# Plain block of an FNet/MLP kernel: first real round on the bare layer norm, scale and shift of the modulation at its eviction

## Chip, core and metric

One core of one Trainium2 chip runs the whole program. The metric is device time in microseconds (us). The kernel before took 1977.84 us, the median of three runs (1975.1 to 1978.34). TensorE is PE, VectorE DVE, ScalarE ACT, GpSimd POOL; SP is the queue that issues most loads.

## What is computed

x is 2048 tokens by 1024 channels; everything is float32 outside.

```python
mod = (_silu(c) @ w_mod).reshape(c.shape[0], 6, 1, -1)
sa, ca, ga, sb, cb, gb = (mod[:, 0], ..., mod[:, 5])
h = _layernorm(x, axis=-1) * (1 + ca) + sa
# _A_ref: a = h @ dft_hid_re.T, b = h @ dft_hid_im.T
#         y = dft_seq_re @ a - dft_seq_im @ b
x = x + ga * _A_ref(h, A_dft_seq_re, A_dft_seq_im, A_dft_hid_re, A_dft_hid_im)
h = _layernorm(x, axis=-1) * (1 + cb) + sb
x = x + gb * _B_ref(h, B_w1, B_b1, B_w2, B_b2)   # gelu MLP, 1024 -> 3584 -> 1024
```

The kernel takes the sequence transform first, so its first products are dft_seq_re times h and dft_seq_im times h.

## The kernel before

Each float32 operand of a product is split into two float16 parts, hi (a rounding, done by ACT) and lo (the rest, done by DVE), and every product is three float16 matmuls: hi by hi, hi by lo, lo by hi (`PASSES`). The stages are: modulation row and layer norm of x; the sequence transform for the first 512 output tokens as a plain block (L1133, `plain1`); the other three groups of 512 tokens by a Strassen-Winograd scheme with seven products (L1183, `winograd1`); the hidden transform (L1415); and the MLP (L1613, L1722).

The plain block is 16 steps. Steps n = 0 to 7 are the real matrix, 8 to 15 the imaginary one. A step uses row tiles k and k+8 of h (k = n % 8) and one coefficient tile, `cop(n)`, and makes 48 matmuls of 128x512: 8 channel groups d (one PSUM bank each), 2 row tiles s, 3 passes. After step 7 the eight banks are evicted by ACT into `uf` (L1112), after step 15 again. Later the kernel needs sums of h tiles for the Winograd scheme (`s_tasks`): four DVE operations (L668 to L671), then hi by ACT (L679) and lo by DVE (L682), stored to DRAM by POOL (L686) from a ring of two buffers, so that the hi of one pair waits for the store of the pair before it.

Before the plain block can begin, h is needed, and h needs sa and ca, that is 8 MB of w_mod. So the program starts with eight loads of 1 MB (L1448). Four of the eight contributions go through PE as float32 matmuls (L485, L507) and four through DVE (L491, L493, summed by L1489); matmuls without use keep PE busy between them (L501). `mod_rows` takes the maximum of the row (L528), makes a power-of-two scale from it and applies it with ca and sa to the first tile. All other tiles go through `x_tasks`: sums by ACT (L622) and squares by ACT (L626), a chain of small operations (L624 to L639), then x minus mean times ca (DVE, L654), times the inverse deviation plus sa (DVE, L655), hi (ACT, L656), lo (DVE, L657). Coefficient tiles are loaded at L713 and split at L702 (ACT) and L705 (DVE). The rows ga, sb, cb, gb are made later (`row_tasks`, L563, L565).

The order on each engine is fixed when the program is built: a planner with costs and due times (`push(stream, tag, tasks, due)`) picks the next task, and each engine then runs its queue in order, stopping wherever an operand isn't there.

## Time and profile before

| | us |
|---|---|
| median of three runs | 1977.84 |
| the profiled execution, its own time | 1974.14 |
| span in the profile | 1972.4 |
| first matmul of the plain block | 34.55 |
| first matmul of the Winograd stage | 208.99 |
| PE busy / DVE busy / ACT busy | 1955.6 / 1421.8 / 851.9 |

PE is the engine to follow: the time is the work of PE and the stretches in which it has none. A busy share of 99% hides two things. Before 34.55 PE is counted as busy with matmuls whose results are thrown away. And matmuls overlap, so that the duration of one (379 ns) is not what it costs; in an undisturbed stretch one starts every 0.216 us.

### The profile page before, as it was taken

What the parts mean: (1) busy time and instruction counts of PE and PEld (TensorE: products, weight loads), DVE (VectorE), ACT (ScalarE), POOL (GpSimd) and SP (SyncE); (2) the same over time, 40 slices, a digit from 0 to 9 for tenths busy, and PEclk for the clock granted to TensorE, in tenths of its full rate; (3) what the DMA queues carried; (4) which work ended last, traced back from release to release, by engine and by line L of the source; (5) the groups of instructions that cost most, each with busy time, mean ns of one, the idle gap of its engine ahead of it and who ended that gap; (6) DMA issues with size and microseconds to landing.
All of it is one profiled execution on the core that took longest, in us unless ns stands there. A gap on an engine that the chain in (4) does not pass through costs nothing.

```text
span 1972.4 us, 23659 instructions
## 1 busy us (share of the span) xinstructions
PE 1955.6 (99%) x9040; PEld 890.5 (45%) x9040; DVE 1421.8 (72%) x1800; ACT 851.9 (43%) x1091; POOL 195.9 (10%) x287
## 2 busy tenths in 40 slices
PE   8999999999999999999999999999999999999999
PEld 3444444444444444444444444444444444444443
DVE  5977888797984477776689998989873453553566
ACT  4743332344542255554576566556323412312311
POOL 0012212221210012211020000000000000000000
PEclk9999999999999999999999999999999999999999
DMA  9158587598788868878954454445476432432324
GB/s 385 63 166 268 184 313 279 211 334 316 252 288 330 304 230 264 279 237 305 353 166 150 187 192 167 151 142 183 175 219 192 125 102 72 133 102 65 113 75 86
DMA packets 139362, 402.41 MB, mean 204 GB/s; under 512 B 15536, under 2 KB 15536, under 8 KB 134640
## 3 DMA queue, kind: packets, MB, share of 16 engines
q1 hardware_dynamic: 111808, 307.30, 46.3%
q0 software_dynamic: 27440, 93.60, 13.3%
q8 instruction: 70, 1.15, 0.2%
q14 instruction: 44, 0.36, 0.1%
HBM read 262.95 MB, written 137.89 MB: 203 GB/s over the span
## 4 chain that ended last, share of the span: by engine, by line
PE 91%; DVE 4%; DMA 2%; ACT 1%; issue 1%; SPq 0%; POOL 0%; DVEq 0%; ACTq 0%; POOLq 0%
PE ps L1613 24%; PE ps L1183 22%; PE ps L1722 22%; PE ps L1415 15%; PE ps L1133 8%; DMA arena<-in_x_dram 1%; DVE arena L409 1%; DVE arena L1768 1%; PE ps L1317 1%; DVE arena L422 1%; ACT arena L397 1%; DMA arena<-in_w_dram 1%; DVE arena L1812 0%; DMA zc<-arena 0%; SPq L1448 0%
## 5 line engine op out<-in xcount | busy, mean ns | idle before, releaser
L1722 PE MATMUL ps<-arena 128*128 128x512 f16 x2352 | 511.3, 379 | 3.4 <-ACT arena L1758 1.4
L1613 PE MATMUL ps<-arena 128*128 128x512 f16 x2352 | 510.4, 379 | 0.0
L1183 PE MATMUL ps<-arena 128*128 128x512 f16 x2016 | 435.3, 379 | 0.0
L1722 PEld LDWEIGHTS <-arena 128*128 128x128 f16 x2352 | 229.9, 98 | 282.5 <-issue 4.8
L1613 PEld LDWEIGHTS <-arena 128*128 128x128 f16 x2352 | 230.2, 98 | 277.0 <-issue 0.3
L1768 DVE SCALAR_TENSOR_TENSOR arena<-ps,i4c,arena 128x1024 f32<-128x1024 f32 x179 | 229.4, 1281 | 145.1 <-PE ps L1722 142.2
L1183 PEld LDWEIGHTS <-arena 128*128 128x128 f16 x2016 | 197.3, 98 | 237.8
L1415 PE MATMUL ps<-arena 128*128 128x512 f16 x1344 | 292.2, 379 | 0.0
L397 ACT ACTIVATE arena<-arena,shc 128x512 f16<-128x512 f32 (+1 forms) x115 | 116.1, 1018 | 281.9 <-PE ps L1722 189.2
L1415 PEld LDWEIGHTS <-arena 128*128 128x128 f16 x1344 | 131.5, 98 | 155.9
L1133 PE MATMUL ps<-arena 128*128 128x512 f16 x768 | 170.1, 384 | 6.5 <-ACT arena L538 2.1
L422 DVE TENSOR_TENSOR arena<-arena 128x512 f32<-128x512 f32 (+1 forms) x228 | 171.0, 753 | 4.2
L702 ACT ACTIVATE arena<-arena 128x1024 f16<-128x1024 f32 x100 | 103.8, 1050 | 155.6 <-PE ps L1183 101.4
L409 DVE SCALAR_TENSOR_TENSOR arena<-arena,shc 128x512 f16<-128x512 f32 (+1 forms) x115 | 128.7, 1122 | 37.4 <-ACT arena L397 37.1
L705 DVE SCALAR_TENSOR_TENSOR arena<-arena 128x1024 f16<-128x1024 f32 x100 | 132.2, 1339 | 26.4 <-ACT arena L702 26.2
L1639 DVE TENSOR_TENSOR arena<-arena,ps 128x512 f32<-128x512 f32 x84 | 57.6, 685 | 109.8 <-PE ps L1613 107.1
L1632 ACT ACTIVATE arena<-arena,b1s,i1c 128x512 f32<-128x512 f32 x84 | 68.3, 813 | 137.6 <-DVE arena L1639 137.6
L1133 PEld LDWEIGHTS <-arena 128*128 128x128 f16 x768 | 75.6, 99 | 100.9 <-issue 6.4
L794 ACT ACTIVATE arena<-arena 128x1024 f16<-128x1024 f32 x56 | 57.4, 1047 | 51.2 <-DMA u<-arena 18.7
L797 DVE TENSOR_TENSOR arena<-arena 128x1024 f16<-128x1024 f32 x56 | 66.9, 1220 | 15.4 <-ACT arena L794 15.4
L397 ACT ACTIVATE arena<-arena,s1c 128x512 f16<-128x512 f32 (+1 forms) x70 | 60.7, 884 | 37.8 <-DVE arena L422 26.2
L409 DVE SCALAR_TENSOR_TENSOR arena<-arena,s1c 128x512 f16<-128x512 f32 (+1 forms) x70 | 66.4, 959 | 10.8 <-ACT arena L397 10.8
(169 smaller groups left out, 1400.2 us busy)
## 6 DMA issues: line engine op xcount, KB each, us to landing
w<-arena SPq DMA_DIRECT2D x64, 512.0 KB, 4.9
arena<-w SPq DMA_DIRECT2D x119, 256.0 KB, 2.7
u<-arena POOLq DMA_DIRECT2D x56, 512.0 KB, 5.4
arena<-u SPq DMA_DIRECT2D x112, 256.0 KB, 3.9
arena<-w SPq DMA_DIRECT2D x56, 512.0 KB, 3.5
arena<-s SPq DMA_DIRECT2D x48, 512.0 KB, 6.4
arena<-in_cre_dram SPq DMA_DIRECT2D x32, 512.0 KB, 7.5
...
```

What stands on the lines that cost most here:

```text
L397: act.activation(o[m][0], q(j), AF.Copy, **sc)
L409: dve.scalar_tensor_tensor(o[m][1], q(j), scale, o[m][0], op0=ALU.mult, op1=ALU.subtract)
L422: dve.tensor_tensor(q(d), q(a), q(b), op=op)
L702: h = Task("act", 1.15, lambda: act.activation(o[:, :, 0], s2, AF.Copy, scale=SC), list(deps) + free)
L705: dve.scalar_tensor_tensor(o[:, :, 1], s2, SC, o[:, :, 0], op0=ALU.mult, op1=ALU.subtract)
L1133: pe.matmul(bank_of(d_), hleft(d_, s, kp, a), cop(n)[:, s, b], start=(kp == 0 and s == 0 and a == 0 and b == 0), stop=(kp == 7 and s == 1 ...
L1183: pe.matmul(bank_of(st + ch), left, cop(n)[:, s, b], start=(start and kp == 0 and s == 0 and a == 0 and b == 0), stop=(kp == 3 and s == 1 ...
L1415: pe.matmul(bank_of(bk), up(N)[:, c_, a], dp(n)[:, c_, w], start=(start and ri == 0 and c_ == 0 and i == 0), stop=(ri == 1 and c_ == 3 and ...
L1613: pe.matmul(ps.rearrange("p (k t) -> p k t", k=4), w1c[:, m, s, a, d * P : (d + 1) * P], zc(m)[:, b, :, d, :], start=(start and d == 0 and ...
L1632: act.activation(dst, src, AF.Gelu_apprx_tanh, scale=inv, bias=b1s[:, 2 * p + j : 2 * p + j + 1])
L1722: pe.matmul(t[:, j], hidc[:, c_, m, a, k * P : (k + 1) * P], w2c[:, m, c_, w], start=(start and c_ == 0 and n == 0), stop=(c_ == 1 and n = ...
L1768: lambda: dve.scalar_tensor_tensor(dst, ps[b], inv, dst, op0=ALU.mult, op1=ALU.add), kp[b],
```

## The change

The first real round works on the bare layer norm, LN(x) times 1024, instead of on h. Since h = LN(x) (1+ca) + sa and the channels are the rows of the result, the product for one channel is (1+ca) times the product with LN(x), plus sa times the sum of the coefficients over the 2048 input positions. So the eviction of the real round scales each partition by a column of 1+ca (`cols`, `evict_plain`), and then DVE adds the coefficient sums times a column of sa (`shift_tasks`). The imaginary round and the Winograd stage still use h. In detail:

- Loads begin with x and coefficient tiles; the eight 1 MB loads of w_mod lie between them (`head`, `tail`), in four buffers.
- All eight contributions of w_mod are summed by DVE (`wm_tasks`); four float32 matmuls with ones, in bank 7, add over the partitions (`mod_sum`) during the real round. Bank 7 is therefore used for d = 7 only after that: the real round runs d = 0 to 6 for all eight steps (42 matmuls each), then d = 7 for all eight (6 each).
- `x_tasks` no longer waits for the row: it normalises x in one operation, on ACT for ten tiles (`ACT_N`), on DVE for six; hi and lo follow.
- New `h_tasks` makes h from LN(x) during the imaginary round: times ca, plus sa, hi, lo for all 16 tiles.
- Eight accumulating loads on POOL sum the coefficients (`csum_tasks`), and two float32 matmuls add over partitions in step 8.
- sa and ca go through DRAM to become columns (`rc_d`, `cols`): 2048 elements of 4 bytes.
- Due times of the later streams move; the loads of `row_tasks` get a stream of their own.

```diff
     def cop(n):
-        return at(O_OP + 4 * (n % 6), 2048, F16).rearrange(...)
+        o = O_OP + 4 * (n % 6 if n < 6 else (n - 8) % 6) if n not in (6, 7) else O_AUX + 12 + 4 * (n - 6)
+        return at(o, 2048, F16).rearrange(...)
...
+    def wm_tasks(k):
+        t = []
+        for h in (1, 0):
+            p = slice(h * D, h * D + D)
+            def f(p=p):
+                if k == 0:
+                    dve.tensor_scalar(rows[:, p], wm2(k)[:, p], scol[:, k : k + 1], None, op0=ALU.mult)
+                else:
+                    dve.scalar_tensor_tensor(
+                        rows[:, p], wm2(k)[:, p], scol[:, k : k + 1], rows[:, p], op0=ALU.mult, op1=ALU.add
+                    )
...
+    def mod_sum(h, n):
...
+        p = rows[:, h * D + 512 * n : h * D + 512 * n + 512]
+        pe.matmul(bank_of(7), ones[:, 0:P], p, start=True, stop=True)
+        t = [Task("act", 0.6, lambda: act.activation(p, bank_of(7), AF.Copy, bias=float(h)), ...)]
...
+    def mod_tasks():
+        t = chain(
+            ("dve", 2.3, lambda: dve.tensor_reduce(mx, rows, axis=AX.X, op=ALU.max, apply_absolute_value=True)),
...
+            ("dve", 0.75, lambda: dve.tensor_scalar(ca1s, rows[:, D : 2 * D], sh, 1.0 / SX, op0=ALU.mult, op1=ALU.mult)),
+            ("dve", 0.75, lambda: dve.tensor_scalar(sas, rows[:, 0:D], sh, None, op0=ALU.mult)),
...
+        a = Task("dma", 1.0, lambda: sp.dma_start(rc_d[:, :], scaled[0:1, :]), ["mod"], "rcs")
+        b = Task("dma", 1.0, lambda: sp.dma_start(cols, rc_d[0].rearrange("(r c p) -> p r c", r=2, p=P)), ["rcs"], "rcl")
...
+    def csum_tasks():
+        for k in range(8):
+            kw = {"accum_op": ALU.add} if k else {}
+            f = lambda k=k, kw=kw: gp.dma_start(csum, cre[0, :, k::8, :], **kw)
...
+    ACT_N = {(4, 0), (7, 1), (3, 1), (6, 1), (7, 0), (5, 1), (3, 0), (5, 0), (6, 0), (4, 1)}
...
+            u = chain(
+                by_act(x_, cl[:, 2, n : n + 1], r) if (k, n) in ACT_N
+                else ("dve", 0.8, lambda: dve.tensor_scalar(x_, x_, mean, r, op0=op, op1=ALU.mult)),
+                ("act", 1.15, lambda: act.activation(hv[:, :, 0], x2, AF.Copy)),
+                ("dve", 1.23, lambda: dve.tensor_tensor(hv[:, :, 1], x2, hv[:, :, 0], op=ALU.subtract)),
+            )
...
+    def h_tasks(k):
-                ("dve", 1.3, lambda x_=x_, mean=mean, op=op: dve.scalar_tensor_tensor(x_, x_, mean, ca1s, op0=op, op1=ALU.mult)),
-                ("dve", 1.3, lambda x_=x_, n=n: dve.scalar_tensor_tensor(x_, x_, r[:, n : n + 1], sas, op0=ALU.mult, op1=ALU.add)),
+                ("dve", 1.23, lambda x_=x_: dve.tensor_tensor(x_, x_, ca1s, op=ALU.mult)),
+                else ("dve", 1.23, lambda x_=x_: dve.tensor_tensor(x_, x_, sas, op=ALU.add)),
...
-    T0 = 42.0
+    T0 = 11.0
...
-        sc = (1.0 - 2.0 * ri) * 2.0**-16
+        sc = -(2.0**-16) if ri else cols[:, 1, d : d + 1]
...
+    def shift_tasks():
+        t = [Task("act", 0.6, lambda: act.activation(rsum, bank_of(7), AF.Copy), ["rs"], "rsum")]
+        for d in range(ND):
+            f = lambda o=o, s=s: dve.scalar_tensor_tensor(o, rsum, s, o, op0=ALU.mult, op1=ALU.add)
...
-                push("u", "u", u_tasks(tb, 0, [[("ev", tb, 1)], [("ev", tb, 6)]]), clk["pe"] + 25.0)
+                push("u", "u", u_tasks(tb, 0, [[("ev", tb, 1)], [("ev", tb, 6)]]), clk["pe"] + -15)
...
+    head = "x0 x8 c0 x1 x9 c1 x2 x10 c2 w0 w1".split()
+    tail = "x3 x11 c3 w2 w3 x4 x12 c4 w4 w5 x5 x13 c5 w6 w7 x6 x14 c6 x7 x15 c7".split()
+    idle_pe(24)
...
-        push("s", "s", s_tasks(k), t_op(8) + 8.0 * k)
+        push("hm", "hm", ab[0], t_op(8 + k) - 25)
+        push("h", "h", ab[1], t_op(8 + k) - 20)
+        push("s", "s", s_tasks(k), T1 - 70 + 7 * k)
...
-    ... row_tasks(...), t_op(16) + 20.0 + 30.0 * n)
+    ... row_tasks(...), t_op(16) + 60.0 + 30 * n)
-        push("row", "row", d_tasks(n), t_op(16 + 28) + 24.0 * n)
+        push("row", "row", d_tasks(n), t_op(16 + 28) + 40 + 22 * n)
```

How the queues change is shown at three places. The line numbers are those of the kernel that a row belongs to. In the changed kernel L496 and L498 are the w_mod products, L652 the layer norm statistics of the first two tiles, L635 the normalisation on DVE and L627 on ACT, L636 hi and L637 lo of LN(x), L667 sums and L671 squares, L744 and L747 hi and lo of the coefficients, L692 and L694 times ca and plus sa, L695 and L696 hi and lo of h, L710 to L713 the four operations of `s_tasks` and L724 its lo, L839 a later split (`u_tasks`).

DVE, from the start of the program, before:

```order
L491 TENSOR_SCALAR arena_65<-arena_65,scol_186 128x2048
L493 SCALAR_TENSOR_TENSOR arena_65<-arena_65,scol_186 128x2048 x2
L493 SCALAR_TENSOR_TENSOR arena_65<-arena_65,scol_186 128x1024 x2
L613 BN_STATS xst_7_190<-arena_65 128x6 x2
L615 BN_AGGR xmv_9_192<-xst_7_190 128x2
```

DVE now, from the normalisation of tile 8 (the fourth operand that PE waits for) on:

```order
L635 TENSOR_SCALAR arena_65<-arena_65,xmv_9_193,xcl_10_194 128x1024
L669 TENSOR_SCALAR xcl_12_196<-xmv_11_195 128x2
L496 TENSOR_SCALAR arena_65<-arena_65,scol_186 128x1024
L637 TENSOR_TENSOR arena_65<-arena_65 128x2x512
L747 SCALAR_TENSOR_TENSOR arena_65<-arena_65 128x2x512
L673 TENSOR_SCALAR xcl_12_196<-xmv_11_195 128x2
L496 TENSOR_SCALAR arena_65<-arena_65,scol_186 128x1024
L617 RECIPROCAL xcl_12_196<-xcl_12_196 128x2
```

The statistics have moved ahead of the w_mod products, and those now stand between the operations of the tiles: the lo of tile 8 (the first L637 here) stands behind the first half product of w_mod.

ACT, in the stretch in which row tiles 5, 13, 6 and 14 are summed, before:

```order
L622 ACTIVATE arena_65,xmv_19_202<-arena_65 128x1024
L626 ACTIVATE arena_65,xmv_17_200<-arena_65,xcl_18_201 128x1024 x2
L656 ACTIVATE arena_65<-arena_65 128x2x512
L622 ACTIVATE arena_65,xmv_19_202<-arena_65 128x1024
L622 ACTIVATE arena_65,xmv_21_204<-arena_65 128x1024
L656 ACTIVATE arena_65<-arena_65 128x2x512
L634 ACTIVATE xcl_18_201<-xcl_18_201 128x2
L702 ACTIVATE arena_65<-arena_65 128x2x512
```

ACT now, in the same stretch:

```order
L667 ACTIVATE arena_65,xmv_19_203<-arena_65 128x2x512 x2
L616 ACTIVATE xcl_18_202<-xcl_18_202 128x2
L671 ACTIVATE arena_65,xmv_19_203<-arena_65,xcl_20_204 128x2x512
L627 ACTIVATE arena_65<-arena_65,xcl_18_202 128x1024
L636 ACTIVATE arena_65<-arena_65 128x2x512
L627 ACTIVATE arena_65<-arena_65,xcl_18_202 128x1024
L636 ACTIVATE arena_65<-arena_65 128x2x512
L671 ACTIVATE arena_65,xmv_19_203<-arena_65,xcl_20_204 128x2x512
L744 ACTIVATE arena_65<-arena_65 128x2x512
```

Two normalisations (L627) have joined the sums, squares and hi parts of a pair of tiles.

DVE, in the last steps of the plain block, before:

```order
L682 TENSOR_TENSOR arena_65<-arena_65 128x2x512 x2
L668 TENSOR_TENSOR arena_65<-arena_65 128x512
L669 TENSOR_TENSOR arena_65<-arena_65 128x512
L670 TENSOR_TENSOR arena_65<-arena_65 128x512
L671 TENSOR_TENSOR arena_65<-arena_65 128x512
L705 SCALAR_TENSOR_TENSOR arena_65<-arena_65 128x2x512 x2
L682 TENSOR_TENSOR arena_65<-arena_65 128x2x512 x2
```

DVE now, there:

```order
L692 TENSOR_TENSOR arena_65<-arena_65 128x1024
L694 TENSOR_TENSOR arena_65<-arena_65 128x1024
L724 TENSOR_TENSOR arena_65<-arena_65 128x2x512
L696 TENSOR_TENSOR arena_65<-arena_65 128x2x512
L747 SCALAR_TENSOR_TENSOR arena_65<-arena_65 128x2x512
L692 TENSOR_TENSOR arena_65<-arena_65 128x1024
L694 TENSOR_TENSOR arena_65<-arena_65 128x1024
L724 TENSOR_TENSOR arena_65<-arena_65 128x2x512
L696 TENSOR_TENSOR arena_65<-arena_65 128x2x512
L710 TENSOR_TENSOR arena_65<-arena_65 128x512
```

Between two lo parts of the sums (L724) now stand the operations on h and its lo (L696, the last is that of the last tile), which the plain block itself needs.

## Rows read from the trace of the kernel before

**Rows 1.** The page: busy us and share of the span, and instructions, by engine

```profile
PE 1955.6 (99%) x9040; PEld 890.5 (45%) x9040; DVE 1421.8 (72%) x1800; ACT 851.9 (43%) x1091; POOL 195.9 (10%) x287
```

**Rows 2.** Busy time by stretch: from:to, us, engines with counts, PEclk, DMA share, GB/s

```profile
34.50:120.00 85.50, 81.11 (x357) 35.53 (x358) 77.74 (x115) 59.36 (x90) 1.27 (x1) 0.96 0.37 131
120.00:209.00 89.00, 89.00 (x414) 40.31 (x412) 63.20 (x67) 38.93 (x45) 21.22 (x39) 1.00 0.73 243
209.00:250.00 41.00, 41.00 (x191) 18.61 (x190) 36.90 (x29) 12.77 (x13) 7.67 (x3) 1.00 0.50 171
...
600.00:700.00 100.00, 100.00 (x465) 45.35 (x464) 46.44 (x56) 27.82 (x35) 8.84 (x15) 1.00 0.78 298
```

**Rows 3.** Timeline of PE from 0 to 60 us: start, us, what, idle before

```profile
34.55 7.04 PE L1133 MATMUL ps<-arena 128*128 128x512 f16 x24 [2.13 <-ACT arena L538]
...
51.83 8.54 PE L1133 MATMUL ps<-arena 128*128 128x512 f16 x31 [1.07 <-DVE arena L705]
```

**Rows 4.** The chain that ended last, in order of time: start, us, what

```profile
51.83 157.15 PE ps L1133 x719
208.99 435.12 PE ps L1183 x2016
```

**Rows 5.** DVE, 0 to 215 us, by form: count, busy us, mean ns, idle before

```profile
L705 DVE SCALAR_TENSOR_TENSOR arena<-arena 128x1024 f16<-128x1024 f32 x22 | 26.5, 1218 | 0.7 <-ACT arena L702 0.7
L682 DVE TENSOR_TENSOR arena<-arena 128x1024 f16<-128x1024 f32 x16 | 19.5, 1224 | 26.6 <-ACT arena L679 26.5
...
L668 DVE TENSOR_TENSOR arena<-arena 128x512 f32<-128x512 f32 x8 | 5.5, 684 | 0.0
...
L528 DVE TENSOR_REDUCE mx<-ps 128x1 f32<-128x512 f32 x4 | 2.7, 690 | 0.3 <-PE ps L507 0.3
L613 DVE BATCH_NORM_STATS2 xst<-arena 128x6 f32<-128x512 f32 x4 | 2.5, 669 | 0.0
L493 DVE SCALAR_TENSOR_TENSOR arena<-arena,scol 128x1024 f32<-128x1024 f32 x2 | 2.5, 1282 | 2.7 <-DMA arena<-in_wm_dram 2.7
...
L563 DVE TENSOR_SCALAR arena<-arena,scol 128x1024 f32<-128x1024 f32 x1 | 0.7, 747 | 0.0
```

**Rows 6.** Timeline of DVE: small chain of one tile; then neighbours in a full queue

```profile
27.05 0.21 DVE L615 BATCH_NORM_AGGREGATE xmv<-xst 128x2 f32<-128x12 f32 x1
...
28.32 0.17 DVE L638 TENSOR_SCALAR xcl<-xcl 128x2 f32<-128x2 f32 x1
...
64.60 1.23 DVE L657 TENSOR_TENSOR arena<-arena 128x1024 f16<-128x1024 f32 x1
65.75 1.28 DVE L655 SCALAR_TENSOR_TENSOR arena<-arena,xcl 128x1024 f32<-128x1024 f32 x1
66.94 1.22 DVE L705 SCALAR_TENSOR_TENSOR arena<-arena 128x1024 f16<-128x1024 f32 x1
```

**Rows 7.** Timeline of ACT, neighbours in a full queue

```profile
59.84 1.04 ACT L622 ACTIVATE arena<-arena 128x1024 f16<-128x1024 f32 x1
...
61.00 1.15 ACT L626 ACTIVATE arena<-arena,xcl 128x1024 f16<-128x1024 f32 x1
...
62.27 1.15 ACT L626 ACTIVATE arena<-arena,xcl 128x1024 f16<-128x1024 f32 x1
...
63.52 1.06 ACT L656 ACTIVATE arena<-arena 128x1024 f16<-128x1024 f32 x1
64.48 1.04 ACT L622 ACTIVATE arena<-arena 128x1024 f16<-128x1024 f32 x1
```

**Rows 8.** Timeline and stretch: first use of a 1 MB load; the load rate

```profile
7.02 1.96 PE L485 MATMUL ps<-arena 128*128 128x512 f32 x4 [1.41 <-DMA arena<-in_wm_dram]
...
15.00:20.00 5.00, 5.00 (x17) 2.20 (x16) 2.35 (x1) 0.00 (x0) 0.00 (x0) 1.00 1.01 421
```

**Rows 9.** Stores of `s_tasks` (L686): us from issue to landing

```profile
DMA to landing us min/median/max: 2.6/6.4/8.8
```

**Rows 10.** DMA issues: what, queue, count, KB each, median us to landing

```profile
cc<-in_c_dram SPq DMA_DIRECT2D x1, 4.0 KB, 1.6
```

394 lines of the change are left out of this document (217 added, 177 removed).

## Prediction

> **What bounds the kernel now.** I read the page by engine first: PE is busy for 1955.6 of 1972.4 us [rows 1], so the question is where PE's work starts and where it stops. The chain that ended last answers for the end: from 51.83 the plain block runs without a stop to 208.99, and from there 2,016 Winograd matmuls take 435.12 us, 0.2158 us each with no gap [rows 4]. What comes before is lost time: the first useful matmul stands at 34.55 [rows 3]. The plain block's 768 matmuls are worth 768 x 0.2158 = 165.7 us and take 208.99 - 34.55 = 174.4; the 8.7 us between are waits in its first two steps and TensorE's clock: 24 matmuls took 7.04 us and, after a stop, 31 took 8.54, where 5.2 and 6.7 would be full speed [rows 3]. Half speed costs 1.9 us each time. Then the other engines: from 34.5 to 120 DVE is busy for 77.7 of 85.5 us, from 120 to 209 for 63.2 of 89, from 209 to 250 for 36.9 of 41, and from 600 to 700 for only 46.4 of 100 [rows 2]. So DVE has some room in the plain block and little right behind it. PE is the bound, DVE is next.
>
> **The change, first part: the start.** The first 1 MB of w_mod is in use at 7.02, and at 421 GB/s a further 1 MB takes 2.5 us [rows 8]. Half a MB of x first means x0 at about 5.8, x8 7.0, c0 8.3, the first w_mod at 18 to 20, the last at 50 to 60. The accumulating loads on POOL start at some 11 us, since nothing holds them back, and share the engines; 4.2 MB are 10 us at that rate, twice that if an accumulating load counts for two, hence the spread. Tile 0 then needs two statistics (0.67 each [rows 5]), the small chain (27.05 to 28.49, plus one more of 0.2 [rows 6]), one normalisation of 0.75 (L563's form [rows 5]) and hi (1.05 [rows 7]): 5.8 + 1.4 + 1.7 + 0.8 + 1.1 = 10.8. The first matmul moves from 34.55 to 10.9, a gain of 23.7 us on the path. PE gets six float32 matmuls in addition; two took 1.96 us with their drain [rows 8], so 0.9 each, 5.4 us, of which 3.5 fall into the real round, beside waits, and 1.7 into step 8, on the path.
>
> **Second part: the real round, where ACT now sets the pace.** In a full queue ACT starts the next instruction 1.16 us after a sum, 1.27 after squares, 0.96 after hi [rows 7]; a normalisation by ACT isn't in the trace; it is the squares without the read of the accumulator, 1.0 to 1.15, and I take 1.1 as its hi waits for it. From the split of c1 (12.3 us) to hi of tile 15 stand 14 sums, 14 squares, 15 hi, 7 coefficients (0.95), 10 normalisations, 8 roots (0.2) and 4 copies from PSUM (0.55): 16.2 + 17.8 + 14.4 + 6.7 + 11.0 + 1.6 + 2.2 = 69.9 us, so 82 at the earliest. It also stops for DVE, whose queue has w_mod products between the operations on tiles. I walked the two queues against each other with these spacings and DVE's: 1.15 for a subtraction, 1.19 for a three-operand operation [rows 6], 1.28 where the next depends on it, 0.7 for half width [rows 5]. Lo of tile 8 waits behind the first w_mod half until 22.0. ACT idles 10.5 us in sum, most of it in three places: 2.0 for the root of tile 1, 2.6 for the squares of tile 6, 2.4 for the last normalisation behind the maximum over 2,048 columns (2.2 us, three times and a bit L528 [rows 5]). Hi of tile 15 ends at 92.5. PE follows the lo parts: tile 8 at 22.0, 1 at 28.2, 2 at 38.4, 4 at 59.4, 5 at 70.4, 7 at 91.7. After that it has 19 + 21 matmuls and the 48 of d = 7 left, 19 us: the real round ends at 110.7 instead of 10.9 + 82.9 + 3.5 = 97.3. Thus 13.4 of the 23.7 us go back.
>
> On clock: a stop has cost 1.9 us here [rows 3]. The Trainium skill ("TensorE: Matmul & The Clock Gate", section "HAM oscillation — how this bites in real kernels") says that a loop with waits between its groups of matmuls is throttled again in every round. By that rule each of some seven stops would cost its 1.9 us; by the walk only the last would, as the others end in a wait for another engine anyway. The sum goes by the walk, and leaves 1.9 us to the range.
>
> **Third part: the imaginary round, where DVE does.** The row is ready when lo of tile 15 and one scaling are done, 94.6. Its way through DRAM to columns is one small store and a load of 4-byte elements; the nearest row is c with 4 KB, 1.6 us [rows 10], from above the slowest store, 8.8 [rows 9]. I take 2.3 + 4. Seven operations on h (8.6 us) fill that time on DVE, and step 8 needs lo of c8 at 107.8, 3 us before PE comes: hidden, with 3 us to spare for the load. The sum of coefficients is long there. Then DVE has, up to lo of the last tile of h: 14 lo and 7 coefficient lo at 1.15, 24 operations with ca or sa at 1.2, 8 shifts and 16 sums at 0.7, 8 lo of sums at 1.15: 24.2 + 28.8 + 16.8 + 9.2 = 79.0 us. That is 186.8, and 2.5 us more, because lo of a sum waits for a store that lands after 6.4 [rows 9] and everything behind it in DVE's queue waits too: 189.3. PE, from 110.7 with 1.7 us for the sum of coefficients, wants this tile after seven steps of 10.36 us, at 185.6. It waits some 3.5 us, and the plain block ends at 110.7 + 1.7 + 82.9 + 3.5 = 198.8.
>
> **Fourth part: behind the plain block.** The first five Winograd operands need 30 us more of DVE (10 half-width sums, 7 + 4 operations of `u_tasks`, 5 coefficient lo, 4 lo of sums), to 220.5 with waits; PE needs them at 198.8, 204.0, 209.2, 214.3 and 219.5, so it stops for 1 to 2 us; up to the tenth operand, near 246, each comes within 1 us of its need. I add 1 us for these. From then on DVE gains on PE again, and the 40 us of work that DVE has more than before (8 half-row w_mod products, 16 x 1.2 for h, shifts) are paid from the 54 idle us between 600 and 700 [rows 2], since the streams of rows and hidden matrices are due 40 us later. Further back the queues are the same instruction by instruction. What stands against the old course: PE is at the state of 208.99 at 201, a **gain of 8 us**. The profiled execution took 1974.14 (span 1972.4 and 1.7 around it); 1966.1 by the sum. Its time lies 3.7 below the median of the runs shown, so the median comes to 1977.84 - 8 = **1969.8**.
>
> **Rivals.** *PE isn't starved in the real round.* If the ACT and DVE stops are half of what I count, the real round ends near 100, DVE starts on h eight to ten us earlier, and with the first wait for tile 8 alone (5 us) the plain block ends at 10.9 + 165.7 + 5.4 + 5 = 187: a gain of 22, 1956. For it: the spacings of rows 7 are full queues, and DVE's sum up to the tenth operand is 218 us, which it could have done by 224. Against: ACT's 69.9 us alone put the last tile past 82.
>
> *DVE eats the gain.* My walk leaves under 1 us at five places behind each other between 185 and 250; 4 to 12 us of waits that I don't see there (the columns at 8.8, a late load) bring PE back to 205 to 213: within 4 us of before, 1974 to 1982.
>
> *The ring of sums becomes the bound; slower.* Before, DVE lost 26.6 us on these stores [rows 5] while PE needed nothing from it. Now hi of a sum, which waits for the store, stands in ACT's queue ahead of hi of h, c15, c16 and evictions, and its lo ahead of lo of h on DVE. The price is the landing: at 8.8 instead of 6.4 us [rows 9], six pairs in a row cost 14 us, PE stands at 215 and the time is 1984. It decides from about 8 to 8.5 us a store, which the loads of the same stretch (0.73 of the DMA engines [rows 2]) could bring about.
>
> The change does what it says: the queues show the first product without a wait for the row, so I give no chance to that it doesn't.
>
> **How the numbers follow.** Forecast, a gain of 4 to 14 us: 0.50. Not starved, 14 to 24: 0.17. Eaten, within 4 us: 0.19. Ring, slower by more than 4: 0.14. About 0.2%, 4 us, is what a measurement of this kernel can tell from no change; so faster 0.67, same 0.19, slower 0.14. The range leaves out the far end of the good case and most of the slow one: 1956 to 1979.
>
> **What the profile will show.** First L1223-type matmul (the plain block's) near 11; PE waiting in the first five steps for hi by ACT and lo by DVE; ACT full from 30 to 92; the first matmul of step 8 near 111; DVE full from 95 to 250; the first Winograd matmul between 196 and 203. Wrong would be: a real round that ends before 103 or after 118; a PE wait for DMA in the first 60 us; evictions that wait for the columns; stops of PE after 260.

## The result, and the profile after

The changed kernel took 1983.6 us (median of 7 runs, 1981.64 to 1990.35), the one before 1975.1 beside it (7 runs, 1973.03 to 1978.34): 1.0048 times the time before, 95% interval 1.0032 to 1.0064. It is slower by some 9 us, where 8 us faster had been forecast, and outside the range. The forecast of 1969.8 started from 1977.84, the median of three runs; the seven runs of the kernel before give 1975.1.

First the page by engine, which answers [rows 1]: PE works 10 us less than before and DVE 40 us more.

```profile
PE 1945.9 (98%) x8996; PEld 884.6 (45%) x8996; DVE 1461.3 (74%) x1849; ACT 875.5 (44%) x1118; POOL 201.3 (10%) x295
```

The timeline of PE up to the end of the plain block (start, us, work, and in brackets the idle time ahead) stands against [rows 3] and the first line of [rows 4]:

```profile
10.76 6.39 PE L1223 MATMUL ps<-arena 128*128 128x512 f16 x21 [2.58 <-ACT arena L636]
...
22.59 34.62 PE L1223 MATMUL ps<-arena 128*128 128x512 f16 x147 [3.94 <-DVE arena L637]
57.96 8.81 PE L1223 MATMUL ps<-arena 128*128 128x512 f16 x40 [0.74 <-DVE arena L637]
...
94.02 26.13 PE L1223 MATMUL ps<-arena 128*128 128x512 f16 x119 [2.00 <-DVE arena L747]
119.99 1.88 PE L1207 MATMUL ps<-arena 128*128 128x512 f32 x4
...
189.48 9.46 PE L1223 MATMUL ps<-arena 128*128 128x512 f16 x43 [0.49 <-DVE arena L696]
```

The first matmul stands at 10.76 instead of 34.55, and the first Winograd matmul at 198.78 instead of 208.82 (so the timeline has it; the chain in [rows 4] begins 0.17 us later). So 10.0 us are won at this point. They are lost behind it. The Winograd stage was one line without a gap, here in the timeline of the kernel before, and is now in pieces:

```profile
208.82 435.28 PE L1183 MATMUL ps<-arena 128*128 128x512 f16 x2016
```
```profile
198.78 36.64 PE L1276 MATMUL ps<-arena 128*128 128x512 f16 x169
236.62 5.34 PE L1276 MATMUL ps<-arena 128*128 128x512 f16 x24 [1.21 <-DVE arena L747]
243.01 46.78 PE L1276 MATMUL ps<-arena 128*128 128x512 f16 x216 [1.05 <-DVE arena L747]
293.18 95.09 PE L1276 MATMUL ps<-arena 128*128 128x512 f16 x432 [3.39 <-DVE arena L747]
392.62 6.81 PE L1276 MATMUL ps<-arena 128*128 128x512 f16 x23 [4.36 <-DVE arena L747]
402.55 105.60 PE L1276 MATMUL ps<-arena 128*128 128x512 f16 x480 [3.12 <-ACT arena L1295]
510.02 145.21 PE L1276 MATMUL ps<-arena 128*128 128x512 f16 x672 [1.87 <-DVE arena L1300]
655.08 45.27 PE L1508 MATMUL ps<-arena 128*128 128x512 f16 x209
```

From its first matmul to the first of the next stage it takes 456.3 us instead of 435.1, 21.2 more: 15.0 are the six stops, some 5.2 are slower matmuls behind the three long ones, and the last 1.0 is the matmul ahead of each stop, which has none behind it to overlap with (379 ns instead of 216). All but one of the stops wait for DVE; L747 splits the low half off a coefficient operand, L1300 is DVE's part of the evictions. The one for ACT's eviction (L1295) goes back to DVE as well: the instruction ahead of it in ACT's queue (L836, 400.54) had waited 4.75 us for DVE. Behind the stage the kernels run alike, 1327.2 us against 1328.5. The account for the profiled executions closes: 10.0 won, 21.2 lost, 1.2 won, 9.9 slower.

What DVE did is seen from the busy times by stretch, in the columns of [rows 2]:

```profile
34.50:120.00 85.50, 79.94 (x359) 35.06 (x357) 68.27 (x104) 64.96 (x89) 6.67 (x6) 1.00 0.60 182
120.00:209.00 89.00, 88.51 (x407) 39.88 (x406) 86.49 (x90) 39.59 (x44) 13.10 (x24) 1.00 0.53 183
...
600.00:700.00 100.00, 100.00 (x465) 45.34 (x464) 45.48 (x43) 25.16 (x28) 7.46 (x14) 1.00 0.92 357
```

From 120 to 209 DVE went from 63.20 to 86.49 of 89 us; from 600 to 700 it did no more than before (45.48 against 46.44). Over the whole Winograd stage, first of the kernel before, then of the changed one (the third pair of numbers is DVE's busy time and its instructions):

```profile
209.00:644.10 435.10, 435.10 (x2017) 197.28 (x2016) 345.90 (x308) 173.93 (x177) 84.67 (x107) 1.00 0.77 279
198.80:655.20 456.40, 441.41 (x2018) 198.47 (x2017) 377.04 (x341) 185.80 (x192) 91.75 (x125) 0.99 0.79 286
```

DVE has 33 instructions and 31 us more to do in the stage: the last three steps of `s_tasks` (L710 to L724, 18 instructions), ten of `u_tasks` (L839, L851), five on coefficients. Before the change these had been done in the plain block, beside DVE's waits there.

The second view is how far DVE is ahead of PE: the operands it has finished, less 16 for the plain block, against PE's matmuls at 24 to an operand. At 387 us of the changed kernel and at 375.4 of the one before, where in each the last of four sums across partitions has just begun or is about to begin on POOL, the counts since the start are (changed kernel first; x is the count):

```profile
L747 DVE SCALAR_TENSOR_TENSOR arena<-arena x51: 1211/1219/5559, 9.8 to 367.6; 128x1024 f16<-128x1024 f32 x51
L1276 PE MATMUL ps<-arena x836: 376/379/631, 198.8 to 386.8; 128*128 128x512 f16 x168
```
```profile
L705 DVE SCALAR_TENSOR_TENSOR arena<-arena x52: 1206/1218/5435, 33.8 to 374.4; 128x1024 f16<-128x1024 f32 x52
L1183 PE MATMUL ps<-arena x772: 379/379/379, 208.8 to 375.2; 128*128 128x512 f16 x193
```

That is 51 - 16 - 836/24 = 0.2 operands ahead now, and 52 - 16 - 772/24 = 3.8 before; one is worth 24 x 0.2158 = 5.2 us. At the stage's start it is 1.0 now and 4.0 before. At the four sums it is 1.3, 3.8, 1.7 and 0.2 now, and 3.8, 2.3, 4.1 and 3.8 before; now PE stops behind the first and the fourth, and before behind none. And a sum on POOL costs DVE several us. The timeline of DVE in the changed kernel, around the first sum (POOL, 282.66, 6.15 us) and the fourth (386.05, 7.01 us):

```profile
281.59 1.22 DVE L851 TENSOR_TENSOR arena<-arena 128x1024 f32<-128x1024 f32 x1
288.84 0.75 DVE L580 TENSOR_SCALAR arena<-arena,m 128x1024 f32<-128x1024 f32 x1 [6.03 <-POOL arena L576]
289.51 2.48 DVE L851 TENSOR_TENSOR arena<-arena 128x1024 f32<-128x1024 f32 x2
291.90 1.22 DVE L747 SCALAR_TENSOR_TENSOR arena<-arena 128x1024 f16<-128x1024 f32 x1
...
385.87 1.22 DVE L851 TENSOR_TENSOR arena<-arena 128x1024 f32<-128x1024 f32 x1
387.01 5.56 DVE L747 SCALAR_TENSOR_TENSOR arena<-arena 128x1024 f16<-128x1024 f32 x1
```

At 282.8 DVE stands for 6.03 us at an instruction that needs the sum, with PE's next operand three instructions behind it; at 387.01 the very split that PE waits for takes 5.56 us instead of 1.22. PE's stops at 293.18 and 392.62 follow. The kernel before has the same sums and the same price, beside the first (POOL, 230.68, 7.02 us) and the fourth (375.47, 8.42 us), and PE does not feel it, being four operands behind:

```profile
230.49 6.69 DVE L705 SCALAR_TENSOR_TENSOR arena<-arena 128x1024 f16<-128x1024 f32 x2
...
387.27 1.23 DVE L584 TENSOR_TENSOR arena<-arena 128x1024 f32<-128x1024 f32 x1 [9.35 <-issue]
```

L584 (L587 in the changed kernel) multiplies the row gb by another row. It needs the fourth sum, a load, and the store of gb, which reads the same memory; the profile names no releaser for its wait. In the changed kernel it stands further back in DVE's queue, at 400.44, and does not wait.

### The profile page after: what moved, and what is told of

Same layout as the page of the kernel before. It is cut to its first block, busy times and chain, and to the rows that moved or that the text cites. A ratio compares the mean times of both kernels' runs of the same rounds, so it can differ in the third digit from the quotient of the medians.

```text
span 1982.3 us, 23620 instructions
## 1 busy us (share of the span) xinstructions
PE 1945.9 (98%) x8996; PEld 884.6 (45%) x8996; DVE 1461.3 (74%) x1849; ACT 875.5 (44%) x1118; POOL 201.3 (10%) x295
## 4 chain that ended last, share of the span: by engine, by line
PE 71%; DVE 3%; issue 1%; DMA 0%; ACT 0%; POOL 0%; DVEq 0%; POOLq 0%; ACTq 0%
PE ps L1709 25%; PE ps L1818 23%; PE ps L1508 15%; PE ps L1276 7%; DVE arena L1864 1%; PE ps L1410 1%; DVE arena L411 0%; DVE arena L779 0%; DVE arena L1908 0%; DVE arena L747 0%; DVE arena L424 0%; DMA arena<-in_w_dram 0%; DMA zc<-arena 0%; POOL zc L1442 0%; ACT ps L958 0%
## 5 line engine op out<-in xcount | busy, mean ns | idle before, releaser
L744 ACT ACTIVATE arena<-arena 128x1024 f16<-128x1024 f32 x100 | 103.4, 1050 | 117.2 <-PE ps L1276 76.5
L747 DVE SCALAR_TENSOR_TENSOR arena<-arena 128x1024 f16<-128x1024 f32 x100 | 129.3, 1305 | 20.7 <-ACT arena L744 20.7
L836 ACT ACTIVATE arena<-arena 128x1024 f16<-128x1024 f32 x56 | 57.8, 1048 | 96.3 <-DVE arena L851 37.5
L839 DVE TENSOR_TENSOR arena<-arena 128x1024 f16<-128x1024 f32 x56 | 67.2, 1218 | 17.0 <-ACT arena L836 17.0
```

Of the source, the lines that this page charges most:

```text
L744: h = Task("act", 1.15, lambda: act.activation(o[:, :, 0], s2, AF.Copy, scale=SC), list(deps) + free)
L747: dve.scalar_tensor_tensor(o[:, :, 1], s2, SC, o[:, :, 0], op0=ALU.mult, op1=ALU.subtract)
```

## The experiments

All times are medians, beside runs of the kernel before on the same chip (1973.3 to 1974.9); "the stage" is the time from the first Winograd matmul to the first of the next stage. The theories at the start: no lead (A), the sums alone (B), the later due times that the change also makes (C).

**The sums across partitions cut to one column.**

```diff
-gp.partition_all_reduce(mrow, mrow, P, RED.add)
+gp.partition_all_reduce(mrow[:, 0:1], mrow[:, 0:1], P, RED.add)
```

> This kernel is the changed one, with the four sums across partitions on POOL (L576, 128x1024, about 7.0 us each) cut to one column, so that four rows of the modulation come out wrong; every instruction stands where it stood. Theory A (no lead: DVE enters the Winograd stage one operand ahead of PE instead of four, so whatever stalls DVE reaches PE): the stalls that hang on the sums go, which are DVE's wait of 6.0 us for the sum at 282.8 and the coefficient splits that took 5.56 (one) and 7.83 us (three) instead of 1.22 each beside a sum; PE's stops at 293.18 (3.39 us) and 392.62 (4.36 us) go with the clock lost behind them, some 2 us each; the stops at 236 and 243 (1.21, 1.05 us) stay. About 1972 us, 1969 to 1976. Theory B (the sums alone make the difference between the kernels): the whole 21 us of the stage go, 1962 to 1964 us. Theory C (later due times of the row products, the d tasks and the u splits make it): no change, 1981 to 1986 us.

Measured: 1970.2 us, 0.9981 (0.9971 to 0.9990) of the time before. The stage takes 442.2, and the stops near 293 and 393 are gone: the second line runs across both.

```profile
244.78 167.52 PE L1276 MATMUL ps<-arena 128*128 128x512 f16 x767 [2.06 <-DVE arena L747]
```

So 13.4 us hang on the sums, as A had it, two thirds of what the stage lost. B, all of it, falls. But the sums cost nothing before; they are the occasion, not what changed.

**The additions of the shift row to h cut to 16 columns, queues unchanged.**

```diff
-dve.tensor_tensor(x_, x_, sas, op=ALU.add)
+dve.tensor_tensor(x_[:, 0:16], x_[:, 0:16], sas[:, 0:16], op=ALU.add)
```

> This kernel is the changed one, with the sixteen additions of the shift row to h (L694, 128x1024, 1.2 us each) cut to 16 columns, so that h comes out wrong; some 18 us of DVE's work go ahead of the Winograd stage, and every instruction stands where it stood. Theory A (no lead): DVE enters the stage three or four operands ahead, as in the kernel before, and the stops at 236, 243, 293 and 393 go, although the sums on POOL and the due times stay; Winograd's 2016 matmuls take 435 to 444 us instead of 456.5, the total is 1964 to 1972 us. Theory B (the sums alone): the stops at 293 and 393 stay, 1979 to 1984 us. Theory C (due times): no change, 1981 to 1986 us.

Measured: 1982.7 us. A in this form falls: 18 us of freed DVE ahead of the stage gave no lead (1.0 at the start). DVE only waits longer in its fixed queue: for L721, which waits for the store ring of the sums of h, 11.7 us from 120 to 200 instead of 1.8.

**The old due times in the changed kernel, and the new ones in the kernel before.**

```diff
-    push("row", "row", row_tasks(j, ...), t_op(16) + 60.0 + 30 * n)
+    push("row", "row", row_tasks(j, ...), t_op(16) + 20.0 + 30.0 * n)
-    push("row", "row", d_tasks(n), t_op(16 + 28) + 40 + 22 * n)
+    push("row", "row", d_tasks(n), t_op(16 + 28) + 24.0 * n)
-    push("u", "u", u_tasks(tb, 0, ...), clk["pe"] + -15)
+    push("u", "u", u_tasks(tb, 0, ...), clk["pe"] + 25.0)
-    push("u", "u", u_tasks(tb, 1, ...), clk["pe"] + 10)
+    push("u", "u", u_tasks(tb, 1, ...), clk["pe"] + 45.0)
```

That is the edit of the first; the second makes it the other way round.

> This kernel is the changed one with the due times of the kernel before for the row products (20 us into the Winograd stage instead of 60), the d tasks and the u splits. Theory C (the later due times crowd DVE's middle): the stage falls back to 435 to 440 us, 1964 to 1968 us. Theory A (no lead): rows that start 40 us earlier fall on a DVE that is one operand ahead, so the stops come earlier and grow, 1984 to 1996 us. Theory B: as the changed kernel within 4 us.

> This kernel is the one before with the due times of the changed one for the row products, the d tasks and the u splits, and nothing else of the change. Theory C: the Winograd stage gets PE stops as in the changed kernel, 1985 to 1996 us. Theory A (no lead): DVE enters the stage four operands ahead all the same, no stop of over 1 us, 1973 to 1979 us. Theory B: the sums are there in both, as before within 3 us.

Measured: 2009.4 us with the old times in the changed kernel, 1984.8 with the new ones in the kernel before. C falls as the whole cause, since undoing it makes things much worse (the stage 483 us). But the new times are no gift: in the kernel before they cost 11.5 us, as much as the whole change, with no more work for DVE in the stage (340 us, before 346). In the profiled execution, the slowest of the four (1991.87), the stage takes 443.9 us, with one stop of 6.41 at the fourth sum: the lead had sunk to 1.1 operands, and L584 was next in DVE's queue, with three instructions between it and PE's next split.

```profile
408.16 1.23 DVE L584 TENSOR_TENSOR arena<-arena 128x1024 f32<-128x1024 f32 x1 [10.67 <-issue]
...
413.98 240.44 PE L1183 MATMUL ps<-arena 128*128 128x512 f16 x1103 [6.41 <-DVE arena L705]
```

**The short addition, planned so.** As above, with the planner's price cut from 1.23 to 0.1 us.

> This kernel is the changed one with the sixteen additions of the shift row to h cut to 16 columns, so that h comes out wrong, and with the planner told so (0.1 us instead of 1.23), so that it lays out the queues anew. In the run that cut them behind the planner's back the operands finished ahead of PE were 1.0 at the stage's start, as in the changed kernel, 1.5 at the first sum and 0.5 at the fourth, and the time stayed. Theory A2 (the operands that DVE has ahead are set by where their splits stand in its fixed queue, and that by the work that the planner has to place ahead of the stage; a stall of DVE costs PE what is over them): told of the free 18 us, the planner puts splits earlier, two or more operands are ahead at the first sum, and the stops of 2 to 5 us at 243, 293 and 393 shrink to under half together; 1967 to 1977 us. Theory D (DVE's load within the stage decides, whatever stood ahead of it): the stage has the same work, the stops near 290 and 390 stay, 1980 to 1985 us.

Measured: 1989.4 us; neither theory's. Up to the third sum it went as A2 said: 672 matmuls from 233.93 on without a stop. Then the fourth sum met a lead of 0.1 operands, with L587 in DVE's queue right behind it, which stood 10.72 us, and PE stopped for 8.87 us.

**Rows later; and operands earlier too.**

```diff
-    push("row", "row", row_tasks(j, ...), t_op(16) + 60.0 + 30 * n)
+    push("row", "row", row_tasks(j, ...), t_op(16) + 70.0 + 40 * n)
-    push("row", "row", d_tasks(n), t_op(16 + 28) + 40 + 22 * n)
+    push("row", "row", d_tasks(n), t_op(16 + 28) + 60 + 22 * n)
```

The second kernel also has the operands' splits due at `t_op(n) - 20.0` instead of 15, and the combinations that feed them 5 us earlier.

> This kernel is the changed one with the four row products due 10, 20, 30 and 40 us later and the d tasks 20 us later; the work is the same. Theory A2: the four sums on POOL move away from the lean stretch, the operands ahead at each of them are over 2, the stops at 293 and 393 go or shrink to 2 us together, those at 236 and 243 stay; 1970 to 1978 us. Theory B (each sum costs PE its 3 to 4 us wherever it stands): as the changed kernel, 1980 to 1986 us.

> This kernel is the one with later rows (row products 10 to 40 us, d tasks 20 us) and has the splits of the operands and the combinations that feed them due 5 us earlier too. Theory A2: about one operand more ahead of PE from 290 on, no stop of over 1 us between 290 and 640; 1966 to 1974 us. Theory B: the sums cost what they cost, 1980 to 1986 us. Theory D: the same load, within 3 us of the kernel with later rows alone.

Measured: 2007.2 and 2005.6 us. The stops moved instead of going (6.95 us at 298 in the first), and the d tasks became late, so that the stage behind waits for their data, ten times in the first:

```profile
672.79 4.44 PE L1508 MATMUL ps<-arena 128*128 128x512 f16 x12 [2.13 <-DMA arena<-dc]
...
697.02 4.44 PE L1508 MATMUL ps<-arena 128*128 128x512 f16 x12 [3.57 <-DMA arena<-dc]
```

This is a fact that the prediction had overlooked: the d tasks cannot be put off much further, because the next stage, from some 655 us on, reads what they leave.

**Half of the additions by accumulating DMAs.**

```diff
-ADD_D = set()
+ADD_D = {(k, n) for k in range(2, 6) for n in range(2)}
```

> This kernel is the changed one with eight of the sixteen additions of the shift row to h made by accumulating DMAs on POOL's queue instead of DVE (k 2 to 5), which the planner counts, so that some 10 us of DVE go ahead of the Winograd stage. Theory A2: half of what leaving out all of them gives, the stops at 236 and 243 go, the others shrink; 1972 to 1980 us, if the eight accumulations of 0.5 MB do not hold up the loads beside them. Theory D: the stops in the stage stay, 1981 to 1986 us.

Measured: 1984.3 us (1980.3 to 1986.4). In the profiled execution, the fastest of the four, the stage falls to 449.9, but it starts at 202.4: hi of h waits 5.2 us for the accumulations. What DVE gives back in the one place is lost in the other.

**Late sums of h in the kernel before** (theory S: the sums of h reach into the stage and take the lead).

```diff
-push("s", "s", s_tasks(k), t_op(8) + 8.0 * k)
+push("s", "s", s_tasks(k), T1 - 50 + 11.0 * k)
```

> This kernel is the one before with the sums of h and their splits (L668 to L682) due 33 to 55 us later, so that they run as late against the Winograd stage as in the changed kernel, where the first pair of stores goes out 44 us ahead of the stage and the last 40 us into it (before: 80 us ahead and 1 us ahead). Nothing else of the change is in it, the due times of the rows are the old ones. Theory S (the sums of h, which the change holds back until h and the shift are there, reach into the Winograd stage; their 17 us of DVE, their waits of some 5 us for a two-buffer ring of stores, and the raw coefficients that need x's memory take the lead of the operands away): operands ahead at the stage's start fall from 4 to 1 or 2, PE stops for 5 us or more in the stage, which takes 440 to 455 us instead of 435; 1980 to 1995 us. Theory C (due times of rows, d tasks and u alone): as before within 3 us.

Measured: 1973.7 us, 0.9995 (0.9986 to 1.0004). S falls: the last of these stores goes out at 237.9, as in the changed kernel, and PE has no stop.

```profile
210.32 435.28 PE L1183 MATMUL ps<-arena 128*128 128x512 f16 x2016
```

DVE had put seven row products in their place ahead of the stage; its work within it stayed at 342.8 us. So late sums of h do no harm by themselves when as much other work goes ahead of the stage.

**A third store buffer.**

```diff
-o = at(O_SO[n], 2048, F16)
+o = at((64, 68, 212)[(2 * k + n) % 3], 2048, F16)      # reuse and slot: 3 back instead of 2
```

The third buffer lies where a load of the row products goes, so the third load of the first row also waits for the last of these stores.

> This kernel is the changed one with three buffers instead of two for the stores of the sums of h; the queues of PE, DVE, ACT and POOL are the same, row by row. Theory S: ACT's wait for these stores (32.3 us between 100 and 240) falls under 10, DVE's wait behind it (5.4 us between 200 and 240) under 1.5, the stops at 236 and 243 go, those at 293 and 393 shrink by some 2 to 3 us each; 1973 to 1980 us. Theory C or D (due times, or the load of the stage): PE's stops at 293 and 393 stay, 1981 to 1985 us.

Measured: 1980.4 us, 1.0033 (1.0021 to 1.0046). The waits went as S said. ACT's for these stores, changed kernel first:

```profile
ACT arena L721 <- DMA s<-arena: 32.3, 8, 8.7
```
```profile
ACT arena L721 <- DMA s<-arena: 3.4, 1, 3.4
```

The stops at 236 and 243 went too. Those at the first and fourth sum stayed (2.91 and 5.35 us). The ring is worth some 3 us; the intervals of the two kernels overlap (the changed one 1.0032 to 1.0064).

**Short addition and short sums together.**

> This kernel is the changed one with the additions of the shift row to h cut to 16 columns and planned so, and with the sums across partitions on POOL cut to one column: h and four rows come out wrong. With the first alone the stage's first 864 matmuls lost 6.4 us instead of 14.1, and 8.9 us went at the fourth sum; with the second alone the total was 1970.2. Theory S with the sums on POOL as the second half: the two losses are separate, only a stop of 2 us near 234 is left, the stage takes 436 to 441 us, 1961 to 1967 us. If both attack the same loss: 1968 to 1972 us.

Measured: 1975.6 us, 1.0004 (0.9994 to 1.0014): 5 us more than with short sums alone. The two do not add. In the new order PE stops at other places (1.83, 1.31, 1.75 us and smaller ones), and DVE waits 23.1 us for the row products' loads.

**d tasks first, rows last.**

```diff
-    push("row", "row", row_tasks(j, ...), t_op(16) + 60.0 + 30 * n)
-    push("row", "row", d_tasks(n), t_op(16 + 28) + 40 + 22 * n)
+    push("row", "row", d_tasks(n), t_op(16) + 80 + 25 * n)
+    push("row", "row", row_tasks(j, ...), t_op(16 + 28) + 120 + 30 * n)
```

The two share buffers, so the waits of their loads are turned round as well, and the next stage's loads wait for the rows.

> This kernel is the changed one with the d tasks ahead of the four row products (d from 80 us into the stage, the rows from 265 us into it), so that the four sums on POOL fall behind 460 us, where four to five operands are ahead of PE, and the d tasks are ready long before 655; the work is the same. Theory B refined (a sum takes 4 to 10 us of DVE and costs PE what is over the lead): the stops at 293 and 393 go, those at 236 and 243 stay, the stage takes 440 to 446 us; 1968 to 1975 us. Theory D (the stage holds more than DVE can do in it): other stops take their place, 1980 to 1990 us.

Measured: 1993.8 us. For 1,320 matmuls from 243.86 on PE has no stop, with five operands ahead from 300 to 400. Then the rows come, the lead falls to 0.2 at 540, and the stops pay for it:

```profile
243.86 286.75 PE L1276 MATMUL ps<-arena 128*128 128x512 f16 x1320 [2.06 <-DVE arena L747]
531.37 10.52 PE L1276 MATMUL ps<-arena 128*128 128x512 f16 x48 [0.77 <-DVE arena L747]
544.79 6.83 PE L1276 MATMUL ps<-arena 128*128 128x512 f16 x24 [2.90 <-DVE arena L747]
```

Theory D was left, that DVE's load in the stage decides. The next runs act on that load directly.

**The row products cut to 16 columns, queues unchanged.**

```diff
-dve.scalar_tensor_tensor(mrow, b, scol[:, k : k + 1], mrow, ...)
+dve.scalar_tensor_tensor(mrow[:, 0:16], b[:, 0:16], scol[:, k : k + 1], mrow[:, 0:16], ...)
```

> This kernel is the changed one with 28 of the 32 row products of the Winograd stage (L571, 128x1024, 1.28 us) cut to 16 columns, so that four rows come out wrong; the loads, the sums on POOL and every queue's order stay. Some 33 us of DVE go out of the stage between 220 and 400. Theory D (in the changed kernel DVE carries 31 us more into the stage, 376.8 us of work instead of 345.9, and the waits in its queue on top no longer fit): the operands get ahead, the sums are covered as in the kernel before, only the stops at 236 and 243 stay; the stage takes 437 to 443 us, 1966 to 1972 us. Theory B (each sum on POOL costs PE its 3 to 4 us): the stops at 293 and 393 stay, 1979 to 1984 us.

Measured: 1977.6 us, the stage 449.9; between the two. The freed time was taken by another wait in the same queue: the products' loads, 15.6 us in the changed kernel, became

```profile
DVE arena L571 <- DMA arena<-in_wm_dram: 36.8, 18, 4.9
```

**25 us more work in the kernel before.**

```diff
+for _ in range(2 if tb < 2 else 1):
     dve.tensor_tensor(o[m][1][1], X(r, h), o[m][1][0], op=ALU.subtract)
```

> This kernel is the one before with the lo parts of u (L797) of the first two blocks of coefficients written twice each: 28 instructions of 1.22 us more on DVE, 7 of them ahead of the Winograd stage and 21, some 25 us, within it between 250 and 430; the order is otherwise the same and the result too. Theory D: the stage gets stops as in the changed kernel, 8 to 20 us, 1982 to 1994 us. If DVE's idle 89 us in the stage take the 25 us up: 1973 to 1977 us.

Measured: 1989.3 us, 1.0073 (1.0058 to 1.0088). DVE's work in the stage is 380.6 us, 34.7 more than before: 21 lo parts (25.6), four operations that had slipped behind the stage's start (L682, L737), and the rest for operations drawn out beside sums. The stage takes 452.4, with two stops, both behind a lead run down to nothing (0.0 operands at 400), one near the fourth sum as in the changed kernel:

```profile
401.30 43.62 PE L1184 MATMUL ps<-arena 128*128 128x512 f16 x192 [5.74 <-DVE arena L705]
451.80 209.50 PE L1184 MATMUL ps<-arena 128*128 128x512 f16 x959 [6.89 <-DVE arena L705]
```

Nothing of the change is in this kernel but the load on DVE, and the loss is the same in kind and nearly in size: the stage is 17.3 us longer, 12.6 of them in the two stops.

**The first six operands split early.**

```diff
-op_tasks(tb, m, kp), t_op(n) - 15.0
+op_tasks(tb, m, kp), t_op(n) - (50 if n < 22 else 15.0)
```

> This kernel is the changed one with the splits of the first six Winograd operands due 50 us ahead instead of 15; the work is the same, the order in DVE's queue changes around the stage's start. Theory A (the lead at the start decides): two or more operands ahead at the start, no stop near 236 and 243, and less at 293 and 393: 1972 to 1978 us. Theory D (the work carried into the stage decides, whoever comes first): the stops move behind 250, 1980 to 1988 us.

Measured: 1999.5 us. The lead at the start rose to 3.0, and was 1.1 ten us later. This order makes no lead that lasts; A in its last form falls.

**The row products emptied**: loads, products and sums, queues unchanged.

```diff
-sp.dma_start(b, wm[:, k, j * D : (j + 1) * D])
+sp.dma_start(b[:, 0:16], wm[:, k, j * D : j * D + 16])      # products as above on 16 columns, sums on 1
```

> This kernel is the changed one with the four row products of the Winograd stage emptied: loads and products of 16 columns, sums across partitions of one column, so that four rows come out wrong; every queue's order stays. Theory D, as a ledger of DVE in the stage (its work plus its waits for DMA, for POOL and for nothing seen): before 373 us in a stage of 435, changed 404 in 456, and all other runs between fall on a line between these. Here some 36 us of products, 12 of slowed work and 25 of waits go: 335 to 345 us. No stop behind 250, those at 236 and 243 stay; the stage takes 436 to 440 us, and the ten us gained at the plain block's end reach the end of the kernel: 1962 to 1967 us. If something else than DVE held the stage, stops near 293 and 393 stay, over 1970 us.

Measured: 1967.8 us, 0.9962 (0.9948 to 0.9975). The stage takes 437.6:

```profile
199.55 36.64 PE L1276 MATMUL ps<-arena 128*128 128x512 f16 x169
237.27 5.34 PE L1276 MATMUL ps<-arena 128*128 128x512 f16 x24 [1.08 <-DVE arena L747]
243.65 393.62 PE L1276 MATMUL ps<-arena 128*128 128x512 f16 x1823 [1.04 <-DVE arena L747]
```

With DVE at 333.1 us of work, no stop is left but the two at 237 and 243, which the store ring makes, and the gain at the head reaches the end.

**Relief without leaving anything out**: three store buffers and the small operations behind a sum on ACT; then twelve of the additions by DMA as well.

```diff
-k_ = Task("dve", 0.9, keep, [s.key])
+k_ = Task("act", 1.15, keep, [s.key])      # act.activation(mrow, mrow, AF.Copy, scale=... / bias=1.0)
-ADD_D = set()
+ADD_D = {(k, n) for k in range(1, 7) for n in range(2)}      # second kernel only
```

> This kernel is the changed one with three store buffers for the sums of h, and with the two small operations behind a sum on POOL (L580, L582: the row times a number, the row plus 1) on ACT instead of DVE, so that ACT, not DVE, stands in a wait for the sum. By the ledger DVE's own time falls from 404 to some 395 us and the stage to 445 to 451 us: 1974 to 1980 us. If DVE is held up beside a sum in any case, the wait only changes its name: as with the third buffer alone, 1979 to 1982 us.

> This kernel is the changed one with three store buffers, the two small operations on ACT, and twelve of the sixteen additions of the shift row to h by accumulating DMAs instead of DVE. Eight of these alone took 11 us off DVE's own time in the stage. By the ledger twelve of them, with the rest, bring it to 380 to 388 us and the stage to 437 to 445 us, with the first Winograd matmul at 200 to 204: 1968 to 1977 us. If the accumulating loads hold up h or the loads beside them: 1978 to 1988 us.

Measured: 1986.7 us for the first, more than either theory allows. Beside the first sum the wait only changed its name: three L851 took 7.95 us instead of 3.5. The fourth shows something else. L587 is not one of the two operations that were moved; in this kernel's order it stands right behind the sum, and waited 9.39 us. PE stopped for 7.13 us ahead of this sum and for 6.20 and 2.99 us behind it, so that the run does not tell what moving the two operations is worth.

```profile
278.99 7.95 DVE L851 TENSOR_TENSOR arena<-arena 128x1024 f32<-128x1024 f32 x3
...
405.71 1.23 DVE L587 TENSOR_TENSOR arena<-arena 128x1024 f32<-128x1024 f32 x1 [9.39 <-issue]
```

The second took 1976.8 us, 1.0008 (1.0000 to 1.0017), 7 us less than the changed kernel and level with the one before. Its Winograd stage takes 445.6 us and starts at 203.3. No version of the changed kernel that does all the work was faster than the kernel before.

The runs side by side, as a ledger of DVE within the stage: "own" is its busy time plus its waits for DMA, for POOL, and for nothing the profile shows, all in us. Waits for ACT and PE (some 40 to 70 us) are left out.

| kernel | busy | waits | own | stage | total |
|---|---|---|---|---|---|
| rows emptied | 333 | 33 | 366 | 438 | 1967.8 |
| new due times, before | 340 | 31 | 371 | 444 | 1984.8 |
| before | 346 | 27 | 373 | 435 | 1975.1 |
| late sums of h, before | 343 | 34 | 377 | 435 | 1973.7 |
| short addition and sums | 355 | 32 | 387 | 444 | 1975.6 |
| short sums | 365 | 28 | 393 | 442 | 1970.2 |
| half of the additions by DMA | 368 | 26 | 393 | 450 | 1984.3 |
| relieved | 368 | 29 | 398 | 446 | 1976.8 |
| short products | 349 | 50 | 399 | 450 | 1977.6 |
| short addition, planned | 359 | 40 | 399 | 459 | 1989.4 |
| u twice, before | 381 | 20 | 401 | 452 | 1989.3 |
| changed | 377 | 27 | 404 | 456 | 1983.6 |
| short addition | 377 | 28 | 405 | 456 | 1982.7 |
| third buffer | 377 | 28 | 406 | 451 | 1980.4 |
| old due times | 382 | 26 | 408 | 483 | 2009.4 |
| buffer and keep | 371 | 38 | 409 | 459 | 1986.7 |
| rows later, operands earlier | 375 | 34 | 409 | 456 | 2005.6 |
| rows later | 375 | 34 | 410 | 459 | 2007.2 |
| d first | 372 | 37 | 410 | 467 | 1993.8 |
| first operands early | 377 | 35 | 412 | 473 | 1999.5 |

Up to some 377 us the stage runs at PE's speed or near it, but for the new due times, where one sum met a short lead. Beyond it the stage grows with DVE's own time, by 0.4 to 1.1 us for each us over 377 up to 406. This is a trend with a wide scatter: near 400 the stage takes 446 to 459 us, and from 408 to 412 it takes 456 to 483. Much of that scatter is between kernels with the same work in another order.

## Why the prediction was wrong

**The start, the real round and the imaginary round were right.** First matmul 10.9 forecast, 10.76 measured. Waits for tile 8 at 22.0 (22.59), tile 4 at 59.4 (57.96), tile 5 at 70.4 (69.42 to 71.64), tile 7 at 91.7 (94.02, where the lo of its coefficient came last). The waits forecast at 28.2 and 38.4 did not appear. The first Winograd matmul was forecast at 198.8 and stands at 198.78. Two misses cancel in this: the real round ends near 113.2 instead of 110.7 (the sum of coefficients at 119.99 has 30 matmuls of step 8 ahead of it, 6.5 us, and the operands of step 7 came 2.3 us late), and the waits for h cost some 0.5 us instead of 3.5. So the agreement to 0.02 us is luck. The columns and the evictions made no wait.

Of the clock neither of the prediction's two readings came out, that each of seven stops costs 1.9 us or only the last. It was low at the start (0.56 from 10.7 to 14, and 21 matmuls took 6.39 us) and behind the stop at 22.59 (0.50 up to 28, so that 147 matmuls took 34.62 us instead of 31.7), and at 1.00 behind the later ones. What it cost lies ahead of waits for ACT and DVE, and the end of the round was not set by it.

**The first five operands cost 2.3 us** (1.21 + 1.05), where 1 us had been added. That is a size, and small. The third buffer, with which both stops went, shows where it is from: the store ring, which the prediction's third rival had named.

**The step that failed is in the fourth part: "From then on DVE gains on PE again, and the 40 us of work that DVE has more than before [...] are paid from the 54 idle us between 600 and 700."** The 40 us were right on the page (1461.3 against 1421.8). They were not paid there: DVE did 45.48 us between 600 and 700, before 46.44. They could not be, for two reasons that the runs show. The work that is put off feeds the stage itself, or, as the d tasks, the stage that starts at 655; put off by 20 us, it stopped PE there. And DVE's idle time within the stage was not free time: 27 of its 89 us before were waits for loads and sums, which come with the work and stay when PE is faster. So 31 us more work went into the stage, and PE paid 15.0 us of stops and 6.2 of what follows them. That load is enough to do this is shown: 25 us added to the kernel before cost 15. The other side is weaker. Emptying the rows takes 18.7 us off the stage, but 14.1 of these go with short sums alone, and short products alone take off 6.4. And load is not the only way to such a loss: the new due times cost the kernel before as much without it.

**The sums on POOL were not in the prediction at all.** They stand in the trace of before as harmless events: two splits beside one took 6.69 us at 230.49, and PE did not wait. Harmless, because of a lead of two to four operands that no step of the prediction measured. With a lead of 1.3 at the first and 0.2 at the fourth they are the places where PE stops; cut short, the four give 13.4 us back. The Trainium skill ("SBUF — State Buffer", section "SBUF: two separate sides") says that VectorE and GpSimd share one pair of ports under an exclusive lock, which an instruction of VectorE with two SBUF inputs needs beside one of GpSimd that reads SBUF, and that the one who comes second blocks until the other's instruction ends. The rows agree in the main: a split, which has two such inputs and takes 1.22 us alone, took 5.56 when it began 0.96 us after a sum of 7.01. Worked out by that rule alone, four sums would have cost DVE up to 28 us in either kernel, which is an estimate. The rows give less: the split ended 0.5 us ahead of the sum's recorded end (spans on POOL are rough), and a sum cost the operations beside it 4.3 to 4.5 us, not 7.0.

**The rivals.** "DVE eats the gain" placed the loss between 185 and 250 and its size at no more than the gain. "The ring of sums becomes the bound" gave 1984, which is the time that came, but not for its reason: PE stood at 198.8 at the plain block's end, not at 215, and a third buffer gives 3 us, not 14. The prediction's own sign of error, "stops of PE after 260", was the one that appeared.

**What stays open.** How much of the 21 us belongs to the load as such and how much to the order that the planner makes of it is not separated: runs with the same work in another order lie between 456 and 483 us of stage. In seven runs (old due times, the planned short addition, rows later, short addition with short sums, d first, first operands early, buffer and keep) the time lay above every range that any theory had been given, and in all seven the order was laid anew. One part of it is L587: where it stood right behind the fourth sum and the lead was short, PE stopped for 6 to 9 us. No run moved it alone. Nor was a sum across partitions on another engine tried.
